# Linear-memory attention and a top-1 mixture of experts on one core: the memory norms read from PSUM, and a list scheduler with new durations and priorities

## The chip, the core and the metric

The kernel runs on one core of a Trainium2 chip. The metric is the device time of one execution in microseconds (us); lower is better. Five engines work beside each other, each through its own queue in order: TensorE (PE in the profile, with its weight loads as PEld), VectorE (DVE), ScalarE (ACT), GpSimd (POOL) and SyncE (SP), which only issues DMA transfers.

## The reference

Two layers follow each other. The first is attention over a local causal window plus a linear memory (4 batches, 8 heads, 576 positions, head width 64). The second sends each of the 2304 resulting rows through one of 8 experts. Cut to what matters:

```
scores = q @ k^T / sqrt(64), causal;  local = softmax(scores) @ v
q_p = phi(q)                           # phi(x) = x+1 where x>0, else exp(x)
mem_ret  = q_p @ M_prev;  mem_norm = q_p @ z_prev + 1e-6
out = g * mem_ret / mem_norm + (1 - g) * local        # g = sigmoid(beta), per head

logits = normalise(x) @ normalise(expert_emb)^T / tau
e = argmax(logits);  gate = softmax(logits)[e]
y = gate * (relu(x @ w1[e]) @ w2[e])
```

## The kernel before

The program has two parts. The second, the expert loop, is written out in a fixed order: 22 slots of up to 128 rows with one expert each, 24 matmuls of the first layer (L1525, in l1c) and 24 of the second (L1602, in l2c) per slot. The first part holds everything else: the attention, the routing of the rows to experts, and three early expert slots, numbered -3 to -1, that start before the last rows are routed. Its order is not written by hand. Each piece of work is an op with a name, an engine, a duration in ns, the ops that it depends on, a priority and the buffers that it takes and frees; the class Sched runs all of them against its own clock, gives each engine the ready op of the lowest priority number among those that can start within a slack, and then emits the instructions in the order of the start times that it planned. Waits between engines are added afterwards, from what each instruction reads and writes. On the chip each engine keeps that order whatever the durations turn out to be.

The attention is cut into 8 groups (a batch and four heads) of 13 units. A unit takes some heads of a block i of 128 queries (i = 0 to 3) or of the last 64 (i = 4) and passes through seven steps: S, the scores on PE (sS: L715, or L690 to L692 for i = 4); M, mask and row minimum on DVE (sM: L718); E, the exponential on ACT (sE: L746, L748); T, transposes on PE (sT: L755, L759); H, the high half of the transposed weights on ACT (sH: L765; L779 for i = 4); L, their low half on DVE (sL: L769); C, the product with v on PE (sC: L804 to L806; L813 for i = 4). The buffer a (4 of them) lives from M to T, aT (5) from H to C. The dictionary po adds to a unit's number to give the priority of each step: a larger number lets the step run later.

Once per group and block, asm_ops joins memory and local part:

- asmM (M_, L896, PE) multiplies phi(q) with the memory into a PSUM bank m of 260 columns: for each of four heads 64 columns of mem_ret and one column of mem_norm. The six PSUM banks of the ring aux serve this and most other steps.
- asmE (E_, L908, ACT) copies m to the SBUF tile ms. The bank is freed.
- d1 (L914, DVE) makes four columns of dd, (mem_norm + 1e-6) / g, out of ms and invg.
- d2 (L922, DVE) makes the other four from the row sums in the bank L of the local part and vsw or invo; rc (L930) inverts all eight columns; xl (L933) scales the local part out of the bank L and frees it.
- A (L939, POOL) scales the memory part out of ms, and ad (L945, POOL) adds both into the row block X.

Then route_ops takes a finished row block: sq (L979, ACT), sc1 and sc2 (L983, L987, DVE), xh (L995 on DVE or L993 on ACT, whichever the scheduler takes), xl (L999 and L1000 on POOL), a transposing DMA, lgm (L1041, L1044 on PE) and lrc (L1050, L1051 on DVE). The last two row blocks go another way: rT (L1024, PE transposes), a copy on ACT or DVE (L1029, L1031), fp32 logits (L1038) and lrc (L1048). batch_ops (L1087 to L1118) ranks the rows on DVE with matmuls on PE (rk, L1099) and scatters their ids on POOL (L1125); tail_ops makes the table of slots on DVE (L1245 to L1294), and gate_ops the gates (chains gn, gl, gr).

The early slots need the first expert's weights as two halves each: the high half on ACT (L1315 for w1, L1327 for w2, four pieces of 1024 columns each), the low half on DVE (L1317, L1329) or POOL (L1318, L1330). The keys nw1l and nw2l say how many of the four pieces DVE takes. Their rows are gathered on POOL (L1453), transposed by a DMA, and widened on ACT (L1506) and DVE (exl, L1509).

Where the scheduler sees a gap on PE of more than some hundred ns, it fills it with small matmuls whose result nobody reads (warm, L255).

## Time and profile before

| | |
|---|---|
| runs, us | 584.61, 587.63, 589.13 (median 587.63) |
| the profiled execution, us | 590.09 |
| its span, first to last instruction, us | 588.4 |
| granted TensorE clock, mean over the span | 0.963 of full speed |
| busy: PE, DVE, ACT, POOL, us | 516.7, 418.1, 312.5, 269.5 |

A busy time is the time in which at least one instruction of the engine ran. All times are in us from the span's start; idle time is what stood before an instruction on its own engine, with what ended it behind the arrow. [...] The attention takes the span up to about 266 us, the expert loop everything from about 316 us on; between them lie the end of the routing and the three early slots.

### The profile page before, as it was taken

The page shows a single profiled execution, that of the slowest core. Times are in us where ns is not written, and L with a number is a line of the kernel's source. Part 1 is how long each engine was busy: PE and PEld are TensorE (multiplying, and loading weights), DVE is VectorE, ACT ScalarE, POOL GpSimd, SP SyncE. Part 2 cuts the span into 40 slices and gives each one's busy share as a digit, 9 for nine tenths or more (in the row PEclk, how much of TensorE's full clock was granted, in tenths as well). Part 3 has the DMA queues.
Part 4 walks back from the last instruction along what each step waited for, and adds up shares of the span by engine and source line. Part 5 has one row for each costly group of instructions (what it writes and reads, how often), then busy time and mean ns, then how long its engine had stood idle before and what let it go on. Part 6 is the DMA issues. An engine that isn't in the chain of part 4 may idle for free. (4 is left out here: it accounts for less than half of the span.)

```text
span 588.4 us, 13339 instructions
## 1 busy us (share of the span) xinstructions
PE 516.7 (88%) x4159; PEld 415.3 (71%) x4159; DVE 418.1 (71%) x1250; ACT 312.5 (53%) x647; POOL 269.5 (46%) x356
## 2 busy tenths in 40 slices
PE   7688899899989989976999999999989899868980
PEld 6577687878676877755776777787767678656760
DVE  5799989699978999978762367444687338962750
ACT  5777777697768786874212246112464125641530
POOL 8556766594956685488542122222320242302110
PEclk9999999899999999999899999999998989999876
DMA  6787264155801432855039237854499745798220
GB/s 132 153 109 176 66 129 112 36 125 114 162 3 41 74 74 11 278 127 108 19 65 347 56 80 207 207 123 85 117 229 296 200 107 131 240 230 217 55 58 13
DMA packets 143769, 75.20 MB, mean 128 GB/s; under 512 B 127928, under 2 KB 128056, under 8 KB 143682
## 3 DMA queue, kind: packets, MB, share of 16 engines
q1 hardware_dynamic: 138882, 63.68, 46.3%
q0 software_dynamic: 4800, 10.52, 6.0%
q8 instruction: 35, 0.57, 0.5%
q14 instruction: 52, 0.43, 0.3%
HBM read 110.69 MB, written 10.67 MB: 206 GB/s over the span
## 5 line engine op out<-in xcount | busy, mean ns | idle before, releaser
L1602 PE MATMUL L<-RC,hhl 128*128 128x512 f32 x504 | 133.2, 423 | 19.7 <-ACT hhl L1569 16.3
L1525 PE MATMUL aux<-RB,xhl 128*128 128x512 f32 x528 | 132.8, 404 | 2.1 <-ACTq L1468 1.1
L1602 PEld LDWEIGHTS L<-RC,hhl 128*128 128x128 f32 x504 | 100.7, 203 | 45.7 <-ACT hhl L1569 17.5
L1525 PEld LDWEIGHTS aux<-RB,xhl 128*128 128x128 f32 x528 | 99.8, 191 | 28.2 <-DVE RB L1404 1.7
L1453 POOL DMA_INDIRECT a<-x_dram,ix x22 | 23.0, 1048 | 151.8 <-DMA ix<-id_dram 130.2
L746 ACT ACTIVATE a<-a,nb 128x128 f32<-128x128 f32 (+3 forms) x128 | 66.4, 562 | 14.6 <-DVE nb L718 11.6
L755 PE MATMUL aux<-ident,a 128*128 128x128 f32 x384 | 62.2, 283 | 7.4 <-ACT a L746 4.1
L718 DVE CUSTOM_DVE_ANT_0 a<-aux,mask 128x128 f32<-128x128 f32 (+3 forms) x144 | 61.4, 448 | 1.5 <-PE aux L755 1.2
L1569 ACT ACTIVATE hhl<-hT 128x1024 fp32r<-128x1024 f16 x18 | 19.0, 1057 | 73.7 <-DMA hT<-h 73.7
L769 DVE SCALAR_TENSOR_TENSOR aT<-aux,aT 128x512 f16<-128x512 f32 (+1 forms) x88 | 55.3, 632 | 3.9 <-ACT aT L765 2.1
L765 ACT ACTIVATE aT<-aux 128x512 f16<-128x512 f32 (+1 forms) x88 | 48.8, 555 | 9.8 <-PE aux L755 5.7
L755 PEld LDWEIGHTS aux<-ident,a 128*128 128x128 f32 x384 | 41.0, 141 | 17.0 <-ACT a L746 11.7
L1615 POOL DMA_INDIRECT out_dram<-ys,ix x22 | 25.1, 1143 | 54.6 <-DVEq L1468 20.3
L806 PE MATMUL L<-vh,aT 128*128 128x65 f16 x320 | 37.4, 194 | 6.2 <-DVE aT L769 5.3
L1535 ACT ACTIVATE hs<-aux 128x512 f32<-128x512 f32 x36 | 21.1, 590 | 37.8 <-PE aux L1525 37.8
L939 POOL TENSOR_TENSOR A<-ms,dd 128x256 f32<-128x256 f32 (+1 forms) x40 | 25.4, 637 | 32.3 <-DVE dd L930 7.9
L804 PE MATMUL L<-vh,aT 128*128 128x65 f16 x320 | 39.3, 195 | 0.4 <-DVE Xl L933 0.4
L805 PE MATMUL L<-vl,aT 128*128 128x64 f16 x320 | 38.9, 193 | 0.7 <-DVE vl L577 0.7
L806 PEld LDWEIGHTS <-aT 128*128 128x128 f16 x320 | 29.5, 98 | 9.1 <-DVE aT L769 7.8
L1400 ACT ACTIVATE RC<-RA 128x1024 fp32r<-128x1024 f32 x24 | 24.7, 1054 | 19.9 <-DMA RA<-in_moe_w_dram 16.1
L804 PEld LDWEIGHTS <-aT 128*128 128x128 f16 x320 | 29.9, 98 | 7.1 <-issue 3.4
L1571 DVE CAST hhl<-hT 128x1024 fp32r<-128x1024 f16 x18 | 12.5, 695 | 27.3 <-DMA hT<-h 26.5
(285 smaller groups left out, 1124.6 us busy)
## 6 DMA issues: line engine op xcount, KB each, us to landing
RA<-in_moe_w_dram SPq DMA_DIRECT2D x172, 512.0 KB
RA<-in_k_dram SPq DMA_DIRECT2D x32, 128.0 KB
RA<-in_q_dram SPq DMA_DIRECT2D x32, 128.0 KB
VN<-in_v_dram SPq DMA_DIRECT2D x32, 128.0 KB
x_dram<-x SPq DMA_DIRECT2D x16, 256.0 KB
hT<-h SPq DMA_TRANSPOSE x36
RA<-in_k_dram SPq DMA_DIRECT2D x8, 64.0 KB
RA<-in_q_dram SPq DMA_DIRECT2D x8, 64.0 KB
```

Source lines behind the costliest of these rows:

```text
L718: nc.vector.tensor_tensor_reduce(out=o, in0=i0, in1=i1, op0=ALU.add, op1=ALU.min, scale=-0.125, scalar=init, accum_out=acc)
L746: nc.scalar.activation(out=a[:, c], in_=a[:, c], func=AF.Exp, scale=-1.0, bias=nb[:, y : y + 1])
L755: nc.tensor.transpose(ps[:, P * y : P * y + P], a[:, P * y : P * y + P], ident)
L765: nc.scalar.activation(out=u["aT"][0:r, o : o + n], in_=t[0:r, 0:n], func=AF.Copy, scale=ASC)
L769: nc.vector.scalar_tensor_tensor(u["aT"][0:r, 640 + o : 640 + o + n], in0=t[0:r, 0:n], scalar=ASC, in1=u["aT"][0:r, o : o + n], op0=ALU.mu ...
L804: nc.tensor.matmul(o, xh, vh[:, kb, hh, :], start=kb == 0, stop=False)
L805: nc.tensor.matmul(o[:, 0:D], xh, vl[:, kb, hh, :], start=False, stop=False)
L806: nc.tensor.matmul(o, xl, vh[:, kb, hh, :], start=False, stop=kb == i)
L939: e.tensor_tensor(st["A"][rr], st["mv"][:, :, 0:D], i1, op=ALU.mult)
L1525: nc.tensor.matmul(G[i]["hp"][n], a[:, cc], w[:, c, 512 * n : 512 * n + 512], start=c == 0 and a is xh and w is w1h, stop=c == KD - 1 and ...
L1602: nc.tensor.matmul(G[i]["yp"], t[a][:, cc], w[:, c, :], start=c == 0 and a == 0 and w is w2h, stop=c == KF - 1 and a == 1)
L1615: nc.gpsimd.indirect_dma_start(out=out[:, :], out_offset=bass.IndirectOffsetOnAxis(ap=G[i]["ix"][:, 0:1].bitcast(U32), axis=0), in_=G[i][" ...
```

## The change

One op changes what it reads. d1 takes the four norm columns straight out of the PSUM bank m instead of ACT's copy ms. It depends on asmM and no longer on asmE, its priority is p0 - 2.0 where it was p0 - 1.0, and the bank is freed when both asmE and d1 are done. The tile dd is allocated in M_. Everything else that is computed stays the same.

The rest sets numbers of the scheduler. Durations: d2 130 to 70 ns, xh on DVE 400 to 500, asmM 440 to 530, lrc 210 to 270, the scatter 1040 to 1270, the gather of the early slots 1040 to 1800, the chain gn 85 to 110, and small additions to S, T and C. Priorities: all of PRIO anew. C goes from -0.27 to 4.90, E from 0.17 to 1.30, H from -1.15 to 0.12, L from -1.06 to 0.92, T from 0.28 to -0.77, S from 0.59 to -0.22, M from -2.5 to -3.09; ra (banks that asmM leaves free) from 2 to 1, rs (the same for S) from 1 to 0, nw1l from 2 to 1, nw2l from 1 to 3, w1p and w2p (the weights' halves), ep (the early slots), and the other offsets by less than 2. A new key re = 1 does for the first layer of the early slots what ra does for asmM.

```diff
         def E_(eng):
             s = SL[ak]
             st["ms"] = wk.tile([P, 260], F32, tag=f"ms{s}", name="ms")
-            st["dd"] = wk.tile([P, 8], F32, tag=f"dd{s}", name="dd")
...
         def d1():
             nc.vector.scalar_tensor_tensor(
-                st["dd"][rr, 0:4], in0=st["mv"][:, :, D : D + 1].rearrange("p h o -> p (h o)"), scalar=1e-6,
+                st["dd"][rr, 0:4], in0=st["m"][rr, 0:260].rearrange("p (h e) -> p h e", e=65)[:, :, D], scalar=1e-6,
                 in1=invg[rr, h4], op0=ALU.add, op1=ALU.mult,
             )
...
-        op(("asmM", gi, i), "PE", 440, M_,
+        op(("asmM", gi, i), "PE", 530, M_,
...
-        op(("d1", gi, i), "DVE", 75, d1, (("asmE", gi, i), ("cg",)), p0 - 1.0)
-        op(("d2", gi, i), "DVE", 130, d2, (("C", lu), ("asmE", gi, i), ("cg",)) + ((((("vs", gi), 3)),) if i < 4 else ()), p0 - 3.5)
+        op(("d1", gi, i), "DVE", 70, d1, (("asmM", gi, i), ("cg",)), p0 - 2.0, free=(bk,))
+        op(("d2", gi, i), "DVE", 70, d2, (("C", lu), ("asmE", gi, i), ("cg",)) + ((((("vs", gi), 3)),) if i < 4 else ()), p0 - 3.5)
...
-            op(("eg", i), "POOL", 1040, lambda i=i: gather(i), (("eix", i),), p0,
+            op(("eg", i), "POOL", 1800, lambda i=i: gather(i), (("eix", i),), p0,
...
-                   alloc=tuple(("aux", ("eh", i, n)) for n in range(2)) if c == 0 else ())
+                   alloc=tuple(("aux", ("eh", i, n), cfg.get("re", 2)) for n in range(2)) if c == 0 else ())
```

What this moves is read from the two programs' instruction orders. In the rows a name's number tells tiles apart, and what stands in brackets is the engine whose work the instruction waits for. The first place is DVE in the second group, at a d1. Before:

```order
L769 SCALAR_TENSOR_TENSOR aT_1304<-aux_1288,aT_1304 128x384 [waits Activation_49]
L718 ISA a0_90,nb_1326<-aux_1296,mask_102 128x512 [waits PE_49]
L718 ISA nb_1326 128x1
L914 SCALAR_TENSOR_TENSOR dd_1309<-ms_1308,invg_130 128x4 [waits Activation_49]
L718 ISA a1_91,nb_1347<-aux_1297,mask_102 128x512 [waits PE_49]
```

Now, at the d1 of the same rank in the order:

```order
L933 TENSOR_TENSOR Xl_1184<-L_1167,dd_1151 128x256 [waits DVE_49,Pool_49]
L718 ISA a0_90,nb_1278<-aux_1242,mask_102 128x512 [waits PE_49]
L718 ISA nb_1278 128x1
L914 SCALAR_TENSOR_TENSOR dd_1275<-aux_1272,invg_130 128x4 [waits PE_49,Pool_49]
L718 ISA a1_91,nb_1297<-aux_1243,mask_102 128x512
```

ACT, now, at the copy of the same bank (aux_1272):

```order
L636 ACTIVATE RA_78<-aux_1233 128x512 x2
L746 ACTIVATE a2_92<-a2_92,nb_1250 128x384 [waits DVE_49,Activation_49]
L908 ACTIVATE ms_1293<-aux_1272 128x260 [waits DVE_49]
L979 ACTIVATE x16_1299,ss_all_140<-X_733 128x512 [waits Pool_49]
L746 ACTIVATE a3_93<-a3_93,nb_1256 128x384 [waits Activation_49]
```

And DVE now, at a d1 of the third group:

```order
L987 TENSOR_SCALAR xsc_142<-xsi_143 128x1 [waits DVE_49]
L769 SCALAR_TENSOR_TENSOR aT_2532<-aux_2505,aT_2532 128x384 [waits Activation_49]
L914 SCALAR_TENSOR_TENSOR dd_2543<-aux_2540,invg_130 128x4 [waits Activation_49,Pool_49]
L769 SCALAR_TENSOR_TENSOR aT_2549<-aux_2514,aT_2549 128x512
L922 SCALAR_TENSOR_TENSOR dd_2473<-L_2456,vsw1_202 128x4 [waits PE_49]
```

Before, each d1 stands behind the copy of its bank and waits for nothing but it. Now both instructions read one bank, and of each pair the one that comes second in the program's order waits for the first: of the 40 pairs, ACT's copy waits for d1 in 11 (as with aux_1272) and d1 waits for the copy in 29 (as with aux_2540).

The second place is PE in the last group, at the units of block i = 2 and the first of i = 3. T is L755, C begins with L804, S is L715, asmM is L896; the units' aT are in their order of T. Before, aT_5017 comes out of aux_5009 and aT_5059 out of aux_5031:

```order
L755 MATMUL aux_5009<-ident_68,a0_90 128x128 x3
L804 LDWEIGHTS aT_4991
L804 MATMUL L_5019<-vh1_87,aT_4991 128x65
...
L755 MATMUL aux_5031<-ident_68,a1_91 128x128 x3
L804 LDWEIGHTS aT_5007
...
L715 MATMUL aux_5047<-RC_80 128x512
...
L804 LDWEIGHTS aT_5017
...
L896 MATMUL aux_5081<-Mb1_95,qp1_82 128x130 x2
L804 LDWEIGHTS aT_5059
...
L755 MATMUL aux_5095<-ident_68,a2_92 128x128 x4
```

Now aT_4911 comes out of aux_4874, and the rows left out are the rest of each step:

```order
L755 MATMUL aux_4874<-ident_68,a0_90 128x128 x3
L804 LDWEIGHTS aT_4760
...
L755 MATMUL aux_4894<-ident_68,a1_91 128x128 x3
L804 LDWEIGHTS aT_4777
...
L715 MATMUL aux_4913<-RC_80 128x512
...
L896 MATMUL aux_4929<-Mb1_95,qp1_82 128x130 x2
L804 LDWEIGHTS aT_4806
...
L755 MATMUL aux_4951<-ident_68,a2_92 128x128 x4
L804 LDWEIGHTS aT_4911
...
L755 MATMUL aux_4971<-ident_68,a3_93 128x128 x4
```

Before, four steps of PE lie between the T and the C of each of these units. Now seven do: by the time of a unit's C, T has transposed two more units behind it. Over the whole program, 227 filling matmuls (L255) stood on PE, and now 135 do: 66 in front of the first scores in both; behind them 161 before and 69 now, 27 of these behind the last L813.

The third place is the end of the attention. PE from its last L813 on, before:

```order
L813 MATMUL L_5312<-VN1_84,aT_5281 64x65 x10
L1525 MATMUL aux_5348<-RB_79,xhl_5301 128x512
...
L1024 MATMUL aux_5365<-ident_68,X_4836 128x128 x4
L1525 MATMUL aux_5348<-RB_79,xhl_5301 128x512
...
L1038 MATMUL aux_5386<-enT32_146,xT_5379 128x8 x4
L1041 MATMUL aux_5394<-enT_145,xT_5346 128x16
...
L1024 MATMUL aux_5403<-ident_68,X4_3643 128x128 x4
L1525 MATMUL aux_5348<-RB_79,xhl_5301 128x512
...
L1038 MATMUL aux_5431<-enT32_146,xT_5421 128x8 x4
L1099 MATMUL aux_5441<-roh_5438,tri_133 128x24
```

Now:

```order
L813 MATMUL L_5145<-VN1_84,aT_5173 64x65 x10
L1041 MATMUL aux_5197<-enT_145,xT_5089 128x16
...
L255 MATMUL aux_5220<-ident16_73 128x128
...
L1024 MATMUL aux_5236<-ident_68,X_4718 128x128 x4
...
L1038 MATMUL aux_5258<-enT32_146,xT_5243 128x8 x4
L1024 MATMUL aux_5263<-ident_68,X4_3721 128x128 x4
...
L1041 MATMUL aux_5282<-enT_145,xT_5214 128x16
...
L1038 MATMUL aux_5292<-enT32_146,xT_5272 128x8 x4
L1525 MATMUL aux_5306<-RB_79,xhl_5268 128x512
...
L1099 MATMUL aux_5326<-roh_5320,tri_133 128x24
```

The first layer of slot -3 (L1525) began right behind the attention and its first three quarters stood between the last two row blocks' transposes and logits; now it stands behind both, and 27 filling matmuls stand in the places between. On POOL, before:

```order
L1000 TENSOR_TENSOR x16_5240<-X_4593,x16_5240 128x512
L945 TENSOR_TENSOR X_4836<-A_5102,Xl_5103 128x256
L1318 TENSOR_TENSOR RB_79<-RA_78,RB_79 128x1024
L939 TENSOR_TENSOR A_5269<-ms_5267,dd_5268 64x256
L945 TENSOR_TENSOR X4_3643<-A_5269,Xl_5270 64x256
L1330 TENSOR_TENSOR RC_80<-RA_78,RC_80 128x1024 x2
L1125 DMA id_dram_76<-idt_132,rpi_5467 19456x2
```

Now:

```order
L1000 TENSOR_TENSOR x16_5171<-X_4473,x16_5171 128x512
L945 TENSOR_TENSOR X_4718<-A_4947,Xl_4948 128x256
L939 TENSOR_TENSOR A_5092<-ms_5091,dd_5076 64x256
L945 TENSOR_TENSOR X4_3721<-A_5092,Xl_5093 64x256
L1318 TENSOR_TENSOR RB_79<-RA_78,RB_79 128x1024 x3
L1125 DMA id_dram_76<-idt_132,rpi_5352 19456x2
```

POOL's adds for the last two row blocks (L945 into X and X4) come before the low halves of w1, of which it now makes three in a row instead of one before and one between; two of the three low halves of w2 that now fall to DVE stand behind the table of slots.

## Rows read from the trace of the kernel before

**Rows 1.** Part 1 of the page: busy time, share of the span and instructions of each engine.

```profile
PE 516.7 (88%) x4159; PEld 415.3 (71%) x4159; DVE 418.1 (71%) x1250; ACT 312.5 (53%) x647; POOL 269.5 (46%) x356
```

**Rows 2.** Busy time by stretch of the span: the stretch and its length, then for each engine busy us and instructions, the granted clock (PEclk), the DMA share and GB/s.

```profile
20.00:264.00 244.00, 219.56 (x2701) 182.10 (x2702) 220.16 (x815) 186.27 (x433) 161.12 (x212) 0.99 0.50 105
264.00:300.00 36.00, 31.28 (x190) 24.91 (x189) 29.65 (x102) 12.68 (x23) 23.72 (x22) 0.91 0.28 53
300.00:588.40 288.40, 252.51 (x1138) 197.27 (x1136) 156.36 (x286) 102.78 (x165) 67.12 (x62) 0.94 0.58 156
...
30.00:90.00 60.00, 54.12 (x660) 44.91 (x660) 56.98 (x214) 45.58 (x111) 39.78 (x50) 1.00 0.66 124
...
108.00:111.00 3.00, 3.00 (x24) 2.88 (x23) 1.90 (x11) 1.28 (x4) 1.71 (x2) 0.50 0.04 8
```

**Rows 3.** Groups of instructions over the whole span, shapes apart: line, engine, operation, out<-in, shapes, count | busy us, mean ns of one | idle us before them and what ended it.

```profile
L914 DVE SCALAR_TENSOR_TENSOR dd<-ms,invg 128x4 f32<-128x4 f32 x32 | 11.5, 359 | 2.1 <-ACT ms L908 1.9 <-issue 0.2
L914 DVE SCALAR_TENSOR_TENSOR dd<-ms,invg 64x4 f32<-64x4 f32 x8 | 2.4, 305 | 0.1
L922 DVE SCALAR_TENSOR_TENSOR dd<-L,vsw 128x4 f32<-128x4 f32 x32 | 4.8, 151 | 0.7 <-PE L L806 0.5
L922 DVE SCALAR_TENSOR_TENSOR dd<-L,invo 64x4 f32<-64x4 f32 x8 | 1.3, 158 | 1.1 <-PE L L813 1.1
L908 ACT ACTIVATE ms<-aux 128x260 f32<-128x260 f32 x32 | 12.3, 385 | 5.3 <-PE aux L896 5.0
L995 DVE TENSOR_SCALAR x<-X,xsc 128x512 f16<-128x512 f32 x13 | 8.8, 681 | 0.4
L1317 DVE TENSOR_TENSOR RB<-RA,RB 128x1024 fp32r<-128x1024 f32 x2 | 2.4, 1218 | 0.0
```

**Rows 4.** The view of one line: count and duration in ns as least/median/longest, then the first and last start.

```profile
L914 DVE SCALAR_TENSOR_TENSOR dd<-ms,invg x40: 104/160/1378, 29.9 to 262.7; 128x4 f32<-128x4 f32 x32, 64x4 f32<-64x4 f32 x8
L922 DVE SCALAR_TENSOR_TENSOR dd<-L,vsw x32: 102/155/163, 29.9 to 260.9; 128x4 f32<-128x4 f32 x32
```

**Rows 5.** Timeline of DVE and POOL near 220 us: start, duration, instruction.

```profile
220.81 1.38 DVE L914 SCALAR_TENSOR_TENSOR dd<-ms,invg 128x4 f32<-128x4 f32 x1
...
220.69 1.47 POOL L673 TENSOR_TENSOR qp<-RA 128x576 f32<-128x576 f32 x1
```

**Rows 6.** Groups of PE in the stretch 20 to 264 us, columns as in rows 3.

```profile
L755 PE MATMUL aux<-ident,a 128*128 128x128 f32 x376 | 60.9, 283 | 7.4 <-ACT a L746 4.1 <-issue 1.6 <-ACT ms L908 0.4
L806 PE MATMUL L<-vh,aT 128*128 128x65 f16 x320 | 37.4, 194 | 6.2 <-DVE aT L769 5.3 <-DVE nr L413 0.5
L255 PE MATMUL aux<-ident 128*128 128x128 f16 x151 | 13.2, 219 | 1.0 <-ACT RA L636 0.8 <-DVE nb L718 0.2
```

**Rows 7.** Timeline: start, duration, instruction, and in brackets the idle time before it and what ended it. The first, two of the middle and the last of the 14 idle pieces of DVE over 0.35 us between 20 and 264 us, and the copy on ACT that the second of them waited for.

```profile
21.73 0.23 DVE L657 TENSOR_TENSOR RC<-aux,RC 128x64 fp32r<-128x64 f32 x1 [2.63 <-ACT RA L636]
...
111.75 0.16 DVE L914 SCALAR_TENSOR_TENSOR dd<-ms,invg 128x4 f32<-128x4 f32 x1 [1.85 <-ACT ms L908]
...
176.28 0.22 DVE L657 TENSOR_TENSOR RB<-aux,RB 128x64 fp32r<-128x64 f32 x1 [3.55 <-ACT aT L779]
...
259.90 0.17 DVE L1050 COPY lrt<-aux 128x8 f32<-128x8 f32 x1 [2.32 <-PE aux L1044]
...
111.33 0.39 ACT L908 ACTIVATE ms<-aux 128x260 f32<-128x260 f32 x1 [1.69 <-PE aux L896]
```

**Rows 8.** Timeline of PE at the end of the attention, columns as in rows 7.

```profile
263.80 2.55 PE L813 MATMUL L<-VN,aT 128*64 128x65 f32 x40
266.28 1.67 PE L1525 MATMUL aux<-RB,xhl 128*128 128x512 f32 x6
...
268.67 1.65 PE L1525 MATMUL aux<-RB,xhl 128*128 128x512 f32 x6
270.66 1.06 PE L1038 MATMUL aux<-enT,xT 128*128 128x8 f32 x8 [0.34 <-ACT xT L1029]
...
272.91 1.64 PE L1525 MATMUL aux<-RB,xhl 128*128 128x512 f32 x6
...
279.38 5.47 PE L1525 MATMUL aux<-RB,xhl 128*128 128x512 f32 x12
284.65 0.24 PE L1099 MATMUL aux<-roh,tri 128*128 128x16 f16 x1
...
288.76 2.97 PE L1525 MATMUL aux<-RB,xhl 128*128 128x512 f32 x12
```

**Rows 9.** Timeline of DVE, ACT and POOL in the same stretch.

```profile
276.04 2.26 DVE L1089 TENSOR_TENSOR req<-req,wdown 128x24 f32<-128x24 f32 x1
...
270.51 1.99 ACT L1327 ACTIVATE RC<-RA 128x1024 fp32r<-128x1024 f32 x2
...
268.38 2.39 POOL L1318 TENSOR_TENSOR RB<-RA,RB 128x1024 fp32r<-128x1024 f32 x1
270.85 0.68 POOL L939 TENSOR_TENSOR A<-ms,dd 64x256 f32<-64x256 f32 x1
271.61 1.05 POOL L945 TENSOR_TENSOR X<-A,Xl 64x256 f32<-64x256 f32 x1
272.74 5.52 POOL L1330 TENSOR_TENSOR RC<-RA,RC 128x1024 fp32r<-128x1024 f32 x2
```

**Rows 10.** From the chain of work that ended last: start, length, what.

```profile
336.99 5.61 PE aux L1525 x24
```

More of the change, by code (lines that the diff above doesn't have):

```diff
@@ L34 @@
 BG = 200.0
-PRIO = {'po': {'S': 0.5860956202798256, 'M': -2.5, 'E': 0.17467982721190245, 'T': 0.2779440791838692, 'H': -1.149000400638553, 'L': -1.05503872663039, 'C': -0.2719843589915537}, 'pa': 0.4405403455875509, 'pv': 10.001535500524492, 'sq': 2.536521872945253, 'xt': 2, 'ra': 2, 'aD': 1, 'ps': 0.775235707503454, 'lv': 2.568625074006147, 'pr': 5.21426841392578, 'rs': 1, 'w1p': 203.44655206520034, 'ag': 0, 'pb': 7.884706576128789, 'lqk': 8.346887064301836, 'rr': 0, 'aA': 1, 'pe4': 1, 'ep': 108.76714709039749, 'w2p': 229.1293559788917, 'slack': 65.79007591242566, 'pp': 1.1250262799121031, 'fc': (), 'nw2l': 1, 'nw1l': 2, 'xlo': 1, 'wpd': 2, 'w1': 300000, 'ND': 2, 'avl': 2, 'ph': 1, 'avc': 1, 'phat': 10154.340622343301, 'ae': 1}
+PRIO = {'po': {'S': -0.2160235072607587, 'M': -3.0899549020790578, 'E': 1.304203441889727, 'T': -0.7657618931148555, 'H': 0.11663590522578293, 'L': 0.9233806848908008, 'C': 4.900025424228725}, 'pa': -0.13743901871318656, 'pv': 9.84168111879135, 'sq': 1.7571266704320558, 'xt': 2, 'ra': 1, 'aD': 1, 'ps': 0.9288269891249477, 'lv': 3.3750164976956643, 'pr': 6.755318923878175, 'rs': 0, 'w1p': 199.9725517826217, 'ag': 0, 'pb': 7.240193326960613, 'lqk': 8.346887064301836, 'rr': 0, 'aA': 1, 'pe4': 1, 'ep': 113.13424642917077, 'w2p': 233.41096144381572, 'slack': 64.63859372264963, 'pp': 0.7987273578081683, 'fc': (), 'nw2l': 3, 'nw1l': 1, 'xlo': 1, 'wpd': 2, 'w1': 300000, 'ND': 2, 'avl': 2, 'ph': 1, 'avc': 1, 'phat': 10154.340622343301, 'ae': 1, 're': 1}
 class Sched:
@@ L831, in unit_ops @@
         if i < 4:
-            dS, dM, dE, dT = max(2 if i == 0 else nh, 1) * 3 * max(111, w / 2.4 + 12) + 150, nh * (c_dve(w) + 8), nh * c_act(w, True), len(u["blocks"]) * e_pe
-            dC = len(u["blocks"]) * (222 if i in FC else 90)
-        else:
-            dS, dM, dE, dT = 3 * (216 + 111), c_dve(512) + 70, c_act(576, True), 5 * e_pe
-            dC = 10 * 116 + 100
+            dS, dM, dE, dT = max(2 if i == 0 else nh, 1) * 3 * max(111, w / 2.4 + 12) + 120, nh * (c_dve(w) + 8), nh * c_act(w, True), len(u["blocks"]) * e_pe + 35
+            dC = len(u["blocks"]) * (222 if i in FC else 90) + (90 if i == 0 else 0)
+        else:
+            dS, dM, dE, dT = 3 * (216 + 111) + 130, c_dve(512) + 70, c_act(576, True), 5 * e_pe + 90
+            dC = 10 * 116 + 150
         p0 = float(n)
@@ L899, in M_ @@
             st["m"] = m
+            st["dd"] = wk.tile([P, 8], F32, tag=f"dd{SL[ak]}", name="dd")
         def E_(eng):
@@ L1056, in route_ops @@
         op(("sc2", key), "DVE", 75, sc2, (("sc1", key),), p0)
-        op(("xh", key), [("DVE", 400, lambda: xh("DVE")), ("ACT", c_act(512, True), lambda: xh("ACT"))][: cfg.get("xt", 2)],
+        op(("xh", key), [("DVE", 500, lambda: xh("DVE")), ("ACT", c_act(512, True), lambda: xh("ACT"))][: cfg.get("xt", 2)],
            deps=(("sc2", key),), prio=p0, free=(xk,))
@@ L1070, in route_ops @@
            alloc=(("aux", ("lg", key), cfg.get("rr", 1)),), free=(("xT", key),))
-        op(("lrc", key), "DVE", 75 if fast else 210, lrc, (("lgm", key), ("sc2", key)), p0 - 0.6, free=(("lg", key),))
+        op(("lrc", key), "DVE", 75 if fast else 270, lrc, (("lgm", key), ("sc2", key)), p0 - 0.6, free=(("lg", key),))
     def batch_ops(bi, keys, p0, prev):
@@ L1133, in batch_ops @@
         for x in range(T):
-            op(("sca", bi, x), "POOL", 1040, lambda x=x: sca(x), d + (("crt",), ("cpadd",)) + tuple(lastld), p0 + 1, xfer=56)
+            op(("sca", bi, x), "POOL", 1270, lambda x=x: sca(x), d + (("crt",), ("cpadd",)) + tuple(lastld), p0 + 1, xfer=56)
             lastsc.append(("sca", bi, x))
@@ L1348, in gate_ops @@
         d += tuple(("sc2", x) for x in T_OF)
-        d = chain("gn", steps, d, p0, dur=85)
+        d = chain("gn", steps, d, p0, dur=110)
         bc = lambda x: x.unsqueeze(2).to_broadcast([P, NT, NE])
@@ L1641, in early_slots @@
             op(("eix", i), "SP", 450, lambda i=i: load_ids(i), (("moff", i),) + tuple(lastsc), p0 - 4 + i, xfer=56)
-            op(("eg", i), "POOL", 1040, lambda i=i: gather(i), (("eix", i),) + ((("exT", i - 4),) if i - 4 >= -NEARLY else ()),
+            op(("eg", i), "POOL", 1800, lambda i=i: gather(i), (("eix", i),) + ((("exT", i - 4),) if i - 4 >= -NEARLY else ()),
                p0 - 4 + i, alloc=(("a", ("ax", i % 4), 0, i % 4),) if i - 4 < -NEARLY else (), xfer=728)
```

## The prediction

> **What bounds the kernel now.** I read the busy shares first, then the same by stretch, then the groups of DVE and PE inside the attention, the idle pieces there, and last the timeline where the attention ends. The shares over the whole span name PE [rows 1]; the reader should not stop there, because the span has two parts with different limits. In the expert loop (300 us on) PE is busy 252.5 of 288.4 us and DVE 156.4 [rows 2]. The change touches nothing in that loop; it can only make it start sooner or later. So the question is how long the attention (20 to 264 us) takes and how long the bridge between it and the loop.
>
> In the attention two engines are level: DVE 220.2 and PE 219.6 of 244 us, 90% each [rows 2]. Of PE's, 151 instructions are fillers that nobody waits for [rows 6]. DVE has no such fill, so DVE is the nearer bound. From 30 to 90 us it is busy 57.0 of 60 us, 95% [rows 2]: the stage can run closer to DVE's limit than it does on average. What holds it below is idle time in 14 pieces of 0.46 to 3.55 us that sum to 17.6 us; most of them wait for ACT or PE [rows 7]. PE in turn waits 7.4 us in front of T, mostly for the exponential, and 6.2 us in front of C's last matmul, mostly for DVE's low half [rows 6].
>
> **The change part by part.** I count against the profiled execution (590.09 us, span 588.4) and carry the difference over to the median, 587.63.
>
> *d1 out of PSUM.* The 40 instructions take 11.5 + 2.4 = 13.9 us, a mean of 359 and 305 ns [rows 3]; but their median is 160 and the longest 1378 [rows 4]. The mean is made by some long ones, and a long one looks like this: d1 starts at 220.81, 0.1 us behind an instruction of POOL with two SBUF inputs, and ends at 222.19 as that one ends at 222.16 [rows 5]. d2 has the same form and size, its first input in PSUM and its second in SBUF: mean 151 and 158 ns, longest 163 [rows 3, 4]. I price the new d1 at d2's rows: 32 x 0.151 + 8 x 0.158 = 6.1 us, so 7.8 us of DVE's time go. The bounds are 0 (the stalls pass to the next instruction) and 9.7 (all at the least duration, 104 ns). With DVE busy 90% of the stage I let 0.9 of it come through: -7.0 us.
> [...]
>
> *A new order inside each pair.* ACT's copy and d1 now read one bank, and in the program the second of each pair waits for the first. In 29 pairs d1 waits for the copy, as before. But before it stood later in DVE's order, and DVE idled only 2.1 us in front of it [rows 3], most of it in one piece [rows 7]. Now the scheduler believes it free as soon as asmM is done and gives it the copy's own priority. If both engines reach the pair together, DVE stands still for the copy's 0.385 us [rows 3] and some 0.03 us from its end to d1's start, as at 111.72 and 111.75 [rows 7], with M and L of other units queued behind. Coming later by chance, it waits less. I take 0.12 us for each, near a quarter of 0.42: 29 x 0.12 = +3.5 us. The bounds are 0 and the 1.85 us seen once. In the other 11 pairs ACT waits for a d1 of 0.15 us; ACT is busy 186 of 244 us, and I take nothing. The longer hold of the bank delays only a later taker of six banks: nothing, up to the same 0.42 us each.
>
> *Work moved off DVE.* One low half of w1 (1.22 us) goes to POOL and two scalings L995 (0.68 each) to ACT [rows 3]: 2.6 us, times 0.9: -2.3 us. ACT's free 58 us cover its part. A gather of the early slots now stands behind more of POOL's routing work; what needs it (exl) comes some 10 us later too, so I take nothing.
>
> *The new order.* Seven steps instead of four between T and C give ACT and DVE more time, so the 6.2 us in front of C [rows 6] should mostly go. They don't add to the terms above, because DVE is the bound: what counts are DVE's own 17.6 us of idling [rows 7]. No row shows the new order, so I bound it by -14 (nearly all of that) and +10 (as much again lost elsewhere), and take a sixth of it, -3.0, because durations nearer to the traced ones leave fewer surprises. The fillers I cost at nothing: they lie in gaps. If the gaps stay without them the clock can fall; in the one half-speed stretch of the attention's middle (three us at 0.50 from 108 us on [rows 2]) PE does half the work, so such a stretch costs up to 1.5 us.
>
> *The bridge.* The attention's PE work ends at 266.35; 18.3 us later, at 284.65, 30 matmuls of the first layer are done [rows 8]. Now the first waits for both last row blocks' logits and for exl. On ACT four high halves of w2 come first (4 x 1.0 us [rows 9]), then the square and the copy; then come PE's 1.1 us of logits [rows 8], DVE's lrc, the low half of the row block and exl. Meanwhile POOL makes three low halves of w1 in a row, 2.39 us each [rows 9], and a DVE instruction with two SBUF inputs stands still until the one in progress ends, as L1089 did (2.26 us, till 278.30, the end of POOL's pair being 278.26 [rows 9]). That puts the first L1525 near 10.7 us behind the attention's end, and with 24 of them (5.61 us [rows 10]) and two ranks between them the first layer of slot -3 is done at about 18.3 us: 24 where there were 30. Six matmuls are +1.4 us. The ends are -4 (the adds into X now come before POOL's low half, which used to delay the last one to 272.66 [rows 9]) and +8.6, below.
>
> Sum: -7.0 + 3.5 - 2.3 - 3.0 + 1.4 = -7.4 us; the profiled execution would be 582.7, the median 580.2.
>
> **The rivals.** *The order closes the gaps.* DVE reaches 92.6%, halfway to the 95% of 30 to 90 us [rows 2]. Its work is 220.2 - 7.8 - 2.6 = 209.8 us, so the stage takes 226.6 instead of 244: -17.4 + 3.5 + 1.4 = -12.5, about 575. For it: the deeper order and the better durations. Against it: the idle pieces come at block changes, which remain.
>
> *The bridge gives it back.* PE starves until exl, and 24 matmuls run at half clock: 12 took 5.47 us at 279 and 2.97 at full clock [rows 8], so 24 lose 5.0; one more low half of POOL in front of exl is 2.2. Then the bridge costs 1.4 + 5.0 + 2.2 = 8.6 and the sum is -0.2: 587.4. For it: the clock fell at this very place before (0.91 on average [rows 2]). Against it: 27 fillers stand there now.
>
> [...] The wait of d1 for the copy is w instead of 0.12 us, because the copy stands behind ACT's own queue: it waited 5.3 us for PE in all [rows 3], and once DVE stood 1.85 us [rows 7]. The attention then changes by -7.0 - 2.3 - 3.0 + 1.4 + 29w. From w = 0.38 on nothing is won, from 0.58 on the kernel is over 1% slower; at w = 0.6 it is +6.5: 594. For it: d1 takes the same priority as the copy, and the model knows nothing of their order. Against it: before, ACT was seldom that late.
> [...]
>
> That d1 goes on stalling in spite of its source I count with the bridge: it leaves +0.4 or so.
>
> **How the numbers follow.** About 1% (5.9 us) is what a measurement of this kernel can tell from no change; the three runs before lie 0.8% apart. Forecast 0.42, of which 0.32 lies below 581.7 and 0.10 within 1%. Gaps closed 0.20, all faster. Bridge 0.24, all within 1%. Pairs 0.14, all slower. So faster 0.52, same 0.34, slower 0.14. The range leaves a tenth on each side: 569 (the order's -14 instead of -3, and none of the bridge's loss) to 592 (half of the pairs' case). The forecast's own range is 575 to 585.
>
> **What would show it.** Right: L914 with a mean near 0.15 us and none over 0.4; the last L813 near 257 us instead of 266; less idle in front of L806; DVE over 91% busy from 20 us to the attention's end; the first L1525 some 8 to 11 us behind the last L813, and the expert loop's first main slot near 309 us. Wrong: idle of DVE in front of L914 of 8 us or more in all (pairs); L995, L577 or L1089 longer by what L914 lost (stalls passed on); a half-speed clock through the first layer of slot -3 (bridge); several half-speed stretches before 250 us (the missing fillers).

## The result, and the profile after

The changed kernel takes 571.21 us (median of 4 runs, 570.86 to 572.55) against 587.77 us for the kernel before, run beside it: a ratio of 0.973 with a 95% interval of 0.969 to 0.977, 16.6 us between the medians. The forecast of 580.2 had the sign and its range held the time, but the gain is more than twice the 7.4 us of the sum. On the chip of the last experiments the same kernel took 579.93 against 589.30 us (0.987, 0.9825 to 0.991), a gain of 9.4 us; where that time lay stands at the end. The experiments ran in five groups, each on a chip of its own. So a difference under some 1.5% between kernels of different groups is not read as one here, and each experiment is told by its ratio to the kernel before on its own chip.

Part 1 of the page of after (it answers to [rows 1]):

```profile
PE 508.6 (89%) x4067; PEld 412.9 (73%) x4067; DVE 409.0 (72%) x1248; ACT 312.0 (55%) x650; POOL 266.6 (47%) x355
```

The span is best cut at two events instead of at fixed times: the end of the attention's last L813 and the start of the first main slot's L1525 (the one that waited for DVE's queue at L1468). Before, in those three stretches (columns as in [rows 2]):

```profile
20.00:266.35 246.35, 221.91 (x2739) 184.38 (x2739) 222.13 (x819) 188.48 (x436) 163.47 (x213) 0.99 0.50 105
266.35:317.15 50.80, 45.15 (x225) 34.77 (x225) 34.79 (x115) 13.16 (x24) 27.49 (x27) 0.93 0.44 110
317.15:588.40 271.25, 236.29 (x1062) 185.13 (x1062) 149.25 (x267) 100.09 (x160) 61.00 (x55) 0.94 0.57 151
```

And after; the fourth row is the 13.6 us of the bridge in which the granted clock was 0.51, the fifth answers to the fourth of [rows 2]:

```profile
20.00:245.77 225.77, 213.34 (x2621) 180.55 (x2622) 210.20 (x817) 187.20 (x438) 159.32 (x212) 0.98 0.54 113
245.77:302.69 56.92, 49.85 (x253) 38.67 (x253) 37.20 (x119) 13.95 (x26) 29.42 (x27) 0.88 0.46 134
302.69:569.30 266.61, 229.88 (x1062) 180.16 (x1062) 149.63 (x267) 99.97 (x160) 60.31 (x55) 0.96 0.58 148
...
251.00:264.60 13.60, 12.55 (x57) 9.98 (x58) 12.35 (x32) 1.81 (x5) 9.48 (x7) 0.51 0.35 78
...
30.00:90.00 60.00, 58.00 (x709) 49.19 (x708) 58.97 (x230) 51.28 (x123) 40.42 (x53) 1.00 0.67 128
```

The attention is 20.6 us shorter, the bridge 6.1 longer, the loop 4.6 shorter: -19.1, the difference of the two spans (the profiled execution of before lies 2.3 us above its median). The loop's code is the same in both; its clock was 0.96 instead of 0.94, and on the last chip it took 271.98 us at 0.94, so its 4.6 us are not shown to be the change's. The reader is to see DVE's column in the first rows: it works 11.9 us less (222.13 to 210.20), and stands idle 8.7 us less (24.22 to 15.57).

The groups of DVE and ACT that answer to [rows 3] and the line views that answer to [rows 4]; L1318 is the low half of w1 on POOL:

```profile
L914 DVE SCALAR_TENSOR_TENSOR dd<-aux,invg 128x4 f32<-128x4 f32 x32 | 5.0, 156 | 4.9 <-ACT ms L908 4.2
L908 ACT ACTIVATE ms<-aux 128x260 f32<-128x260 f32 x32 | 12.5, 395 | 9.7 <-PE aux L896 4.1 <-POOL A L939 3.5 <-DVE dd L914 1.7
L995 DVE TENSOR_SCALAR x<-X,xsc 128x512 f16<-128x512 f32 x11 | 9.4, 858 | 0.7 <-POOL X L945 0.5
L1318 POOL TENSOR_TENSOR RB<-RA,RB 128x1024 fp32r<-128x1024 f32 x3 | 7.6, 2561 | 0.1
...
L914 DVE SCALAR_TENSOR_TENSOR dd<-aux,invg x40: 140/158/166, 22.3 to 239.7; 128x4 f32<-128x4 f32 x32, 64x4 f32<-64x4 f32 x8
```

No d1 is longer than 166 ns. And PE in 20 to 264 us, which answers to [rows 6]: the wait in front of C's last matmul has gone from 6.2 to 1.4 us.

```profile
L755 PE MATMUL aux<-ident,a 128*128 128x128 f32 x376 | 60.2, 284 | 5.7 <-DVE Xl L933 3.2 <-ACT a L746 1.3 <-DVE n L411 0.4
L806 PE MATMUL L<-vh,aT 128*128 128x65 f16 x320 | 37.2, 195 | 1.4 <-DVE aT L769 1.1 <-DVE nr L414 0.3
L255 PE MATMUL aux<-ident 128*128 128x128 f16 x66 | 5.9, 226 | 0.0
```

Between 20 us and the attention's end DVE now has seven idle pieces over 0.35 us (8.7 us in all) where before had 14 (17.6; four of them stand in [rows 7]). Two are long: 2.18 us at the end, and this one, from the timelines of DVE, ACT and POOL. d1 waited for the copy, the copy for POOL to give a buffer back, and POOL for a DMA:

```profile
226.62 0.16 DVE L914 SCALAR_TENSOR_TENSOR dd<-aux,invg 128x4 f32<-128x4 f32 x1 [3.98 <-ACT ms L908]
...
226.20 0.39 ACT L908 ACTIVATE ms<-aux 128x260 f32<-128x260 f32 x1 [3.51 <-POOL A L939]
...
225.56 0.61 POOL L939 TENSOR_TENSOR A<-ms,dd 64x256 f32<-64x256 f32 x1 [7.31 <-DMA id_dram<-idt,rpi]
```

The bridge, which answers to [rows 8, 9]: PE, DVE and POOL.

```profile
244.39 1.38 PE L813 MATMUL L<-VN,aT 128*64 128x65 f32 x20 [1.16 <-ACT aT L779]
255.95 2.05 PE L1525 MATMUL aux<-RB,xhl 128*128 128x512 f32 x4
...
260.46 4.78 PE L1525 MATMUL aux<-RB,xhl 128*128 128x512 f32 x12
...
250.93 2.59 DVE L995 TENSOR_SCALAR x<-X,xsc 128x512 f16<-128x512 f32 x1 [0.48 <-POOL X L945]
...
253.69 2.59 DVE L1004 SCALAR_TENSOR_TENSOR x<-X,xsc,x 128x512 f16<-128x512 f32 x1
256.21 2.61 DVE L1509 CAST xhl<-xT 128x512 fp32r<-128x512 f16 x1
...
250.89 7.61 POOL L1318 TENSOR_TENSOR RB<-RA,RB 128x1024 fp32r<-128x1024 f32 x3
```

Three instructions of DVE (L995, L1004, L1509), each beside one of POOL's three low halves, take 2.6 us each.

### The profile page after: what moved, and what is told of

It reads as the page before. It is cut to its first block, busy times and chain, and to the rows that moved or that the text cites. A ratio compares the mean times of both kernels' runs of the same rounds, so it can differ in the third digit from the quotient of the medians.

```text
span 569.3 us, 13194 instructions
## 1 busy us (share of the span) xinstructions
PE 508.6 (89%) x4067; PEld 412.9 (73%) x4067; DVE 409.0 (72%) x1248; ACT 312.0 (55%) x650; POOL 266.6 (47%) x355
## 5 line engine op out<-in xcount | busy, mean ns | idle before, releaser
L1602 PE MATMUL L<-RC,hhl 128*128 128x512 f32 x504 | 127.3, 408 | 23.3 <-ACT hhl L1569 17.3
L1525 PE MATMUL aux<-RB,xhl 128*128 128x512 f32 x528 | 133.7, 406 | 3.5 <-ACTq L1468 1.0
L1602 PEld LDWEIGHTS L<-RC,hhl 128*128 128x128 f32 x504 | 95.5, 193 | 48.6 <-ACT hhl L1569 18.5
L1525 PEld LDWEIGHTS aux<-RB,xhl 128*128 128x128 f32 x528 | 100.2, 193 | 30.0 <-DVE RB L1404 2.0
L755 PE MATMUL aux<-ident,a 128*128 128x128 f32 x384 | 61.9, 287 | 5.7 <-DVE Xl L933 3.2
L755 PEld LDWEIGHTS aux<-ident,a 128*128 128x128 f32 x384 | 43.1, 144 | 15.4 <-ACT a L746 11.1
L806 PE MATMUL L<-vh,aT 128*128 128x65 f16 x320 | 37.2, 195 | 1.4 <-DVE aT L769 1.1
L804 PE MATMUL L<-vh,aT 128*128 128x65 f16 x320 | 38.0, 197 | 0.0
L804 PEld LDWEIGHTS <-aT 128*128 128x128 f16 x320 | 30.0, 98 | 4.8 <-issue 3.6
L939 POOL TENSOR_TENSOR A<-ms,dd 128x256 f32<-128x256 f32 (+1 forms) x40 | 24.6, 618 | 18.3 <-DMA id_dram<-idt,rpi 7.3
L1404 DVE TENSOR_TENSOR RC<-RA,RC 128x1024 fp32r<-128x1024 f32 x24 | 28.3, 1220 | 6.2 <-ACT RC L1400 5.8
```

The costliest lines, as they stand in the source:

```text
L755: nc.tensor.transpose(ps[:, P * y : P * y + P], a[:, P * y : P * y + P], ident)
L804: nc.tensor.matmul(o, xh, vh[:, kb, hh, :], start=kb == 0, stop=False)
L806: nc.tensor.matmul(o, xl, vh[:, kb, hh, :], start=False, stop=kb == i)
L1404: nc.vector.tensor_tensor(l, s, h.bitcast(F32), op=ALU.subtract)
L1525: nc.tensor.matmul(G[i]["hp"][n], a[:, cc], w[:, c, 512 * n : 512 * n + 512], start=c == 0 and a is xh and w is w1h, stop=c == KD - 1 and ...
L1602: nc.tensor.matmul(G[i]["yp"], t[a][:, cc], w[:, c, :], start=c == 0 and a == 0 and w is w2h, stop=c == KF - 1 and a == 1)
```

## The experiments

Two theories stood at first. A: the new order carries the gain, and d1's source adds little. B: the source carries it, since each stall held up a late chain. "New order" is what the scheduler makes of the table and the durations. To compare sources without another order, a few kernels take the finished order of one kernel as it is and only move the d1 that the data force: ahead of the next taker of the bank, or behind the copy. A distance "from T to C" below is PE's work between a unit's transposes and its C, worked out from PE's order with the traced mean durations: median 2.14 us before and 4.08 after, under 2 us in 45 and 7 of 104 units.

**The source, in either order, and the two parts of the scheduler's input alone** (one chip, before 587.75 us).

```
psum_old_order, in before:   - in0=st["mv"][:, :, D:D+1]...      + in0=st["m"][rr, 0:260]...[:, :, D]
copy_new_order, in after:    - in0=st["m"][rr, 0:260]...[:, :, D] + in0=st["mv"][:, :, D:D+1]...
table_only, in before:       - PRIO = {old}   + PRIO = {new}, and the line that reads its key re
durations_only, in before:   the diff's changed durations alone
```

> The order of before, instruction for instruction, with d1 reading PSUM; 15 of the 40 d1 come earlier on VectorE, ahead of the next taker of their bank. L914 should have a mean near 0.15 us with none over 0.4. My sum's first term alone: -7.0 us against before, about 581. Theory A (the new order carries the gain; a stall of d1 in the old order mostly lay in time that VectorE then idled anyway): -1 to -4 us. Theory B (a stall of up to 1.4 us holds up a late chain, so the source is worth more than its busy time): -8 to -12 us.

> The order of after, with d1 reading ScalarE's copy again; only the 11 d1 that stood ahead of their copy move behind it. L914 back to a mean of 0.3 us or more with some over 1 us. Theory A: 3 to 7 us slower than after, 574 to 578, so the order keeps -10 or more of the 16.4. Theory B: 10 us or more slower than after, 581 or more.

> Before with the new table of priorities alone (with the number of banks that slots' first layer keeps free), the old durations, d1 from the copy. Here PE has 3.97 us of other work between a unit's T and its C in the median, against 2.14 before and 4.08 in after. Theory A1 (that distance carries the gain): 573 to 579. Theory A2 (the durations carry it): 584 to 590. Theory B: 584 or more.

> Before with the new durations alone, the old table, d1 from the copy. The distance from T to C stays short, 2.09 us in the median. Theory A1: 584 to 592, no gain. Theory A2 (better durations leave fewer surprises): 575 to 581.

Measured: 587.0 (ratio 0.998, 0.9945 to 1.002), 587.2 (0.999, 0.996 to 1.002), 585.7 (0.995, 0.992 to 0.998) and 599.6 us (1.017, 1.012 to 1.022). Neither theory fits all four: psum_old_order is near A and far from B, copy_new_order lies in B's range and outside A's, and the loss of durations_only was foreseen by none. No part alone gives more than 0.5%, and the durations alone cost 1.7%. In the old order the source did what was forecast to L914, and the attention still got no shorter:

```profile
L914 DVE SCALAR_TENSOR_TENSOR dd<-aux,invg x40: 102/150/166, 30.0 to 263.6; 128x4 f32<-128x4 f32 x32, 64x4 f32<-64x4 f32 x8
...
20.00:267.87 247.87, 225.56 (x2739) 189.99 (x2739) 217.19 (x819) 188.91 (x436) 163.87 (x213) 0.97 0.49 104
```

DVE is busy 4.9 us less than before in that stretch, and idle 6.5 us more: what the stall had taken, the next wait takes. Part of that may be this one execution, which lies 3.0 us above its median and had a lower clock in the attention than the trace of before (0.97, there 0.99); that nothing was won rests on the medians of 12 and 29 runs. So term one of the sum is right for DVE's work and worth nothing by itself in the old order. copy_new_order had put two things back, the read of SBUF and 11 waits for the copy (8.0 us of DVE's idling in 11 times), so its loss does not yet say which of them matters.

**Which of the two it was** (another chip, before 586.0 us). Theory C: the new order leaves DVE no idle time, so a stall shows in full. Theory D: the 11 waits did it. Theory E: the distance from T to C is what lets the gain through.

```
copy_29:          src = st["m"]... if nm in EARLY (the 11) else st["mv"]
psum_behind_copy: for the 11 d1 ahead of their copy: order.remove(d); order.insert(order.index(copy) + 1, d)
near_c_new_order: each C moved ahead on PE, no further than what it needs, until T to C is 1.7 us in the model
late_c_psum_old_order: each C of the first seven groups moved back on PE, no further than what needs it, until 3.5 us
```

> The order of after, instruction for instruction; the 29 d1 that stand behind their copy read the copy, the 11 that stand ahead of it read PSUM. So the reads of SBUF come back without any new wait. If d1's stalls behind GpSimd are exposed in the new order (theory C: the order took away VectorE's idle time, so nothing hides a stall any more): 6 to 10 us slower than after, 577 to 581. If the loss of copy_new_order came from the 11 waits for the copy (theory D): within 3 us of after, 569 to 574.

> The order of after, all 40 d1 reading PSUM, but the 11 that stood ahead of their copy moved behind it. No read of SBUF, 11 new waits. Theory C: 3 to 6 us slower than after, 574 to 577 (VectorE stood 8.0 us in front of L914 in copy_new_order, 4.2 in after). Theory D: 10 us or more slower, 581 or more.

> The order of after with each C moved ahead on PE until some 2 us of PE's work lie between T and C (2.10 us in the median, 44 of 104 units under 2 us, as in before; 4.08 and 7 in after); the other engines' orders stay. Theory E (the longer distance from T to C is what lets d1's gain through): PE waits 4 us or more in front of L806 again, and the time is 578 to 586. Rival (the rest of the order carries it): 569 to 576.

> The order of before with d1 out of PSUM, as psum_old_order, and each C of the first seven groups moved back on PE as far as its takers allow, to some 3.5 us of PE's work behind T (3.78 us in the median, 11 units under 2 us); the other engines' orders stay. Theory E: 574 to 582, most of the change's gain with nothing but d1's source and the place of C. Rival (the rest of the order carries it): 584 to 590.

Measured: 574.5 (0.980, 0.973 to 0.987), 571.4 (0.976, 0.968 to 0.984), 593.1 (1.012, 1.005 to 1.018) and 602.9 us (1.028, 1.020 to 1.037). Either half alone costs little: 0 to 3 us against after's first run, which is less than groups of runs differ by, and 3.1 us between the two, whose intervals overlap. So D falls, and C had forecast more than came for both (577 to 581 and 574 to 577). In the traces the read of SBUF alone (copy_29) makes the attention 4.3 us longer than after's, the waits alone (psum_behind_copy) 2.7, and the two together made 15.5 in copy_new_order: the delays don't add, and that sum is not explained by either (part may be the chip). near_c_new_order is clear: with C moved on PE and nothing else, it takes 21.7 us more than psum_behind_copy on the same chip (which is after but for the place of 11 d1), more than E had forecast, and the wait that the prediction had named comes back. The first row is psum_behind_copy's, the second near_c_new_order's, over each one's attention:

```profile
L806 PE MATMUL L<-vh,aT 128*128 128x65 f16 x320 | 37.2, 195 | 2.4 <-DVE aT L769 1.5 <-DVE dd L914 0.4 <-DVE nr L414 0.3
```

```profile
L806 PE MATMUL L<-vh,aT 128*128 128x65 f16 x320 | 38.7, 196 | 18.4 <-DVE aT L769 14.4 <-DVE dd L922 1.4 <-DVE dd L914 0.6
```

The other way round E failed (574 to 582 forecast): a later C in the old order took PE's wait away (0.8 us) and gave DVE one, since d2 stands in DVE's queue where C used to end. Groups of late_c_psum_old_order:

```profile
L806 PE MATMUL L<-vh,aT 128*128 128x65 f16 x320 | 35.7, 195 | 0.8 <-DVE aT L769 0.8
...
L922 DVE SCALAR_TENSOR_TENSOR dd<-L,vsw 128x4 f32<-128x4 f32 x32 | 5.1, 160 | 18.6 <-PE L L806 18.4
```

**The parts by twos, the tail moved with C, and the fillers** (a third chip, before 585.23 us). all_but_d1 is after with the lines of d1 as before; table_and_d1 is before with the table and the d1 edit; late_tail_psum gives each C before 205 us of the scheduler's time, and the five operations behind it, a start 2 us later in the old order; no_fillers_new_order sets `self.warm_to = 0.0`.

> Table and durations of after, d1 as in before (from the copy, after it, and the scheduler knows that). All that the change moves but for d1; from T to C 4.08 us. If the gain is the order's and copy_new_order lost it only by the way in which d1 was put back: 573 to 579. If the new order needs d1 out of the way (theory C): 581 to 588, as copy_new_order.

> Before with the new table and the whole d1 edit, with the old durations. From T to C 3.82 us. Theory C (long distance and d1 out of PSUM are what it takes, the durations are a detail): 571 to 578. Rival F (the table fits only the durations that it was set for; any part missing gives back most): 581 to 590.

> The order of before with d1 out of PSUM, and each C before 205 us of the scheduler's time given a start 2 us later, now with what follows it (d2, the reciprocal, Xl, A and the add) by as much on its engine; dependences and buffers as they were, all else in place. From T to C 3.81 us in the median instead of 2.14. In late_c_psum_old_order VectorE stood 18.4 us in front of d2 because d2 had stayed; that should go. Theory E (distance, with the engines' orders matching it): 574 to 582. Rival F: 585 or more.

> After without its 135 filler matmuls, every engine's order else the same. If the clock of the attention doesn't hang on them, 569 to 573; the bridge, where 27 of them stand, would show it first. If it does: half-speed stretches before 245 us and 574 to 582.

Measured: 577.8 (0.989, 0.984 to 0.9935), 574.6 (0.984, 0.979 to 0.989), 610.4 (1.045, 1.039 to 1.052) and 572.3 us (0.978, 0.973 to 0.982). The last stands for after on this chip, having its order: so table and durations give 7.4 of some 13 us, and the d1 edit on top of them, with the order that it brings, 5.5. Theory C fits table_and_d1 (571 to 578) but not all_but_d1 (581 to 588), so d1 out of PSUM is not what the new order needs in order to gain at all. As a recipe theory E is refuted: with its tail moved too, a later C makes things worse still. The square, the routing and the transposes behind the adds into X had stayed where they were, and the waits now stand in front of them. Groups of late_tail_psum's attention (POOL's add, then ACT, DVE and PE behind it):

```profile
L979 ACT ACTIVATE x<-X 128x512 f32<-128x512 f32 x16 | 10.1, 631 | 9.6 <-POOL X L945 7.3 <-DMA x_dram<-x 2.4
...
L983 DVE TENSOR_SCALAR xsi<-ss_all 128x1 int32<-128x1 int32 x16 | 2.4, 149 | 9.1 <-ACT x L979 9.1
...
L1041 PE MATMUL aux<-enT,xT 128*128 128x16 f16 x60 | 3.9, 174 | 7.6 <-DMA xT<-x 7.4
```

In these runs the distance was worth something only in the order that the scheduler had made with it in every queue. The fillers are worth about nothing in the attention (clock 0.98 with and without, 226.64 us against 225.77) and some 3 us in the bridge (59.97 against 56.92), by one trace each from two groups of runs; after itself may thus be a little faster on the third chip than its stand-in. Behind a gap of PE the clock was low in both kernels: before, PE was busy 0.44 of the 2 us from 104 us on, and the clock was 0.50 from 108 to 111 us; after, PE was busy 0.41 of the 2 us from 247 us on, and the clock was 0.50 from 251 to 262 us.

**The last two pairs, and the bridge** (a fourth chip, before 591.91 us). d1_edit_alone and durations_and_d1 keep the old table. The other two change `nw1l` in after's table from 1 to 4 (w1's low halves on DVE), no_low_on_gpsimd also `nw2l` from 3 to 4.

> Before with the whole d1 edit (PSUM, behind the product and not the copy, the copy's priority), old table, old durations; from T to C 2.06 us. It completes the table of the three parts with none 587.8, table 585.7, durations 599.6, table and durations 577.8, table and d1 574.6, all three 571.2. If d1's gain needs the long distance: 584 to 592. If d1's place in the order is what psum_old_order lacked: 578 to 583.

> After with the old table: the new durations and d1 edit; from T to C 2.11 us. If the distance, which only the table sets, carries the order's gain: 586 to 600, the durations costing here too. If the durations pay once d1 is out of the way: under 582.

> After with all four low halves of w1 on VectorE (three were on GpSimd, 7.6 us in a row from 250.89 us on, beside L995, L1004 and L1509 of 2.59 us each); attention and its order as in after. One low half of w2 on GpSimd moves into their place. Theory G (these stalls delay the bridge): first L1525 6 to 8 us behind the last L813 instead of 10.2, the bridge 3 to 5 us shorter, 566 to 569. Rival H (the three halves on VectorE, 3.7 us, cost there what the stalls did, or the loop's clock gives it back): 570 to 573.

> As w1_low_on_vector, and the last low half of w2 on VectorE too, late in the bridge: no low half left on GpSimd. Theory G: 1 to 2 us less again, 565 to 568, with L995, L1004 and L1509 all under 1 us. Rival H: 570 to 574.

Measured: 600.7 (1.016, 1.0095 to 1.023), 598.1 (1.014, 1.007 to 1.022), 572.0 (0.967, 0.961 to 0.973) and 573.6 us (0.971, 0.966 to 0.977). The two with the old table lose, d1_edit_alone more than either guess. The two with fewer low halves on POOL lie in H's ranges by their times, but this chip was the slowest for before, and after did not run on it, so they do not decide; taking the last low half of w2 off POOL gave nothing on top. With the first three groups this fills the square of the three parts, as ratios to before on the same chip:

```
                    no d1 edit            d1 edit
old table           1                     1.016
old table, new dur. 1.017                 1.014
new table           0.995                 0.984
new table, new dur. 0.989                 0.973 (0.978 third chip, without fillers; 0.987 fifth)
```

Under the old table each new input alone costs some 1.6%, and both together 1.4%: there the losses do not add either. Under the new one the d1 edit gains where like runs beside like (0.989 and 0.978 on the third chip, intervals apart). The gain of the durations lies within the intervals on that chip (0.984 and 0.978), and beside the fifth chip's 0.987 neither gain would be seen.

**Whether the shorter bridge is a gain** (a fifth chip, both kernels side by side, before 589.30 us).

> The changed kernel once more, on one chip with w1_low_again: about 571, and 2.7% under before.

> w1_low_on_vector once more: in its profile the bridge was 5.3 us shorter (51.6 for 56.9) while the attention of the same order ended 6.0 us later. Theory G (the shorter bridge is a gain, the attention's end differed by the execution): 3 to 5 us under after_again. Rival H (what the bridge wins is lost again): within 2 us of after_again.

Measured: 579.93 (0.987, 0.9825 to 0.991) and 574.44 us (0.977, 0.972 to 0.982). w1_low_again is 5.5 us under after on the same chip, and the intervals don't meet: it is the best version of this study, and H falls. Where the time went is another matter. First the three stretches of after_again, then those of w1_low_again:

```profile
20.00:250.88 230.88, 216.94 (x2621) 183.08 (x2620) 208.86 (x813) 188.03 (x438) 159.63 (x212) 0.97 0.53 110
250.88:306.62 55.74, 49.77 (x253) 38.62 (x254) 37.41 (x119) 13.96 (x26) 29.78 (x27) 0.88 0.47 138
306.62:578.60 271.98, 235.22 (x1062) 184.24 (x1062) 149.73 (x267) 100.14 (x160) 61.43 (x55) 0.94 0.56 145
```

```profile
20.00:254.07 234.07, 218.14 (x2621) 184.06 (x2621) 213.34 (x816) 189.02 (x439) 161.38 (x213) 0.97 0.50 110
254.07:304.41 50.34, 46.80 (x254) 37.29 (x254) 31.27 (x120) 12.95 (x25) 22.48 (x23) 0.92 0.50 142
304.41:573.80 269.39, 234.67 (x1062) 182.73 (x1062) 149.35 (x267) 99.78 (x160) 61.62 (x56) 0.95 0.56 147
```

The bridge is 5.4 us shorter and the attention 3.2 longer: the three low halves that DVE took over now start before the attention's end and take 5.6 us there (L1317 below), so part of the bridge's gain is work moved in front of the cut. DVE's three stalled instructions are gone but for L1004, which still stands beside the one low half of w2 that POOL kept:

```profile
248.18 3.30 DVE L1317 TENSOR_TENSOR RB<-RA,RB 128x1024 fp32r<-128x1024 f32 x2
252.53 2.29 DVE L1317 TENSOR_TENSOR RB<-RA,RB 128x1024 fp32r<-128x1024 f32 x1
...
257.95 0.49 DVE L995 TENSOR_SCALAR x<-X,xsc 128x512 f16<-128x512 f32 x1
259.17 2.83 DVE L1004 SCALAR_TENSOR_TENSOR x<-X,xsc,x 128x512 f16<-128x512 f32 x1
261.92 0.41 DVE L1509 CAST xhl<-xT 128x512 fp32r<-128x512 f16 x1
...
259.10 2.35 POOL L1330 TENSOR_TENSOR RC<-RA,RC 128x1024 fp32r<-128x1024 f32 x1
```

Slot -3's first layer begins no sooner for it, at 262.45 us against 261.38 in after_again:

```profile
261.38 2.05 PE L1525 MATMUL aux<-RB,xhl 128*128 128x512 f32 x4
```

```profile
262.45 2.91 PE L1525 MATMUL aux<-RB,xhl 128*128 128x512 f32 x6
```

The main slot starts 2.2 us sooner, and the other 2.6 of the 4.8 us between the two spans lie in the loop, whose code is the same and whose clock was 0.95 for 0.94; the bridge's clock was 0.92 for 0.88. So the gain came, a little larger than theory G said, but its reason, that the stalls delay the bridge, is not shown: the clock may have given as much.

## Why the prediction was wrong

The failed step is the term "The new order": "They don't add to the terms above ... take a sixth of it, -3.0". DVE's work was forecast well: -7.8 for d1 and -2.6 moved off, 10.4 us, against 11.9 measured. Its idling was not: with an attention 8.8 us shorter (-7.0 + 3.5 - 2.3 - 3.0) the sum let DVE idle 1.6 us more, and it idles 8.7 less. Those 10.3 us are nearly all of the 11.8 by which the attention (-20.6) was missed. The mechanism written down beside the term, more time between T and C, is the one that near_c_new_order shows to be needed; for want of a row I gave the new order a sixth of DVE's 17.6 us of idle pieces, and the trace gives half of them, even with the pairs' new wait among them. The reason given for the sixth, durations nearer to the traced ones, is not borne out: alone they cost 1.7%. By the runs of the third chip both halves of the sum were too small: table and durations, for which it has -3.9 (-2.3 - 3.0 + 1.4), gave 7.4 us, and the d1 edit, for which it has -3.5 (-7.0 + 3.5), gave 5.5 on top of them.

How far the sum missed differs between the groups of runs as well. In the last one the whole gain was 9.4 us, near the forecast's 7.4; but even there the attention took 230.88 us, 15.5 less than in the trace of before (from another chip), and it was the loop that won nothing.

- *d1 out of PSUM, -7.0*: the removal is as said (13.9 to 6.3 us, least to longest 140 to 166 ns; nothing moved into L577, whose mean fell from 0.85 to 0.79 us; L995's rose from 681 to 858 ns, by the one of 2.59 us in the bridge). "I let 0.9 of it come through" is wrong as a share of its own: nothing came through in the old order (psum_old_order); in the new one the source alone is worth some 3 us that the intervals don't separate from nothing (copy_29 against psum_behind_copy), and the whole d1 edit 5.5 (all_but_d1 against no_fillers_new_order). The source hardly shows in d1's median: 158 ns from PSUM against 160 before from SBUF, and in copy_29 161 (11 from PSUM) against 163 (29 from SBUF).
- *A new order inside each pair, +3.5*: DVE idles 4.9 us in front of the 32 full d1 where it idled 2.1, +2.8. The size is right, the form is not: 3.98 of it is the single piece at 226.62, which came from POOL's buffer and not from a late ACT. psum_behind_copy has 7.8 us of such waits and loses no time against after's first run.
- *Work moved off DVE, -2.3*: in the attention L1317 and L995 take 1.6 us less (9.4 before, 7.8 now), not 2.6. That DVE's work fell by more than forecast all the same is due to L577 (1.1 us less) and an L1509 that moved into the bridge (0.6), which the sum did not have.
- *The bridge, +1.4* (the traces, not the medians): the first L1525 starts 10.2 us behind the attention's end (10.7 forecast), but the 24th matmul is done at 21.0 instead of 18.3, at a granted clock of 0.51 up to 264.6 us, as the bridge's rival had it; the whole bridge is +6.1. The loop won 4.6 back, its clock 0.96 for 0.94, so that from the attention's end to the kernel's the sum is +1.5: right in total by luck, from two errors.
- *Rivals*: "the order closes the gaps" is what happened; it said DVE at 92.6% and 575 us, and it is 93.1% (210.20 of 225.77). I gave it 0.20 because the idle pieces at block changes would remain; of 14 pieces seven are left. "The bridge gives it back" came in part. The pairs' case fell: 2.8 us over 29 pairs is w = 0.10.
- *What would show it*: the last L813 ended 11 us earlier than said, the main slot started at 302.69 instead of 309; the other signs of being right were as named. Of the signs of being wrong one came, the half-speed clock in the first layer of slot -3 (0.51 from 251.0 to 264.6 us; its first matmul began at 255.95).

What stays open: why the two halves of copy_new_order lose 12 us more together than each alone, how much of it is the chip, and why durations and d1 cost time under the old table and not under the new one: the distance from T to C is shown to be needed, not to be enough.

## What to carry to other kernels

A cost removed from one queue is worth what the order around it lets through; in psum_old_order the queue handed the freed time to the next wait. So don't add a scheduler's edit and its new order as two terms, but ask how far the best stage already runs (95% of DVE from 30 to 90 us stood in the profile) and give that ceiling its weight. A table of priorities belongs to the inputs it was set for: here the three kernels that changed durations or a dependence under the old table lost 1.4 to 1.7%. Look for POOL's instructions with two inputs in a row before giving work to POOL: here, in after, an instruction of VectorE took 2.6 us beside each of three (L995, L1004 and L1509).
